# Splitting the last load of V by rows, and exchanging two closing copies, in a decode kernel

## The chip, the cores and the metric

The kernel runs on one core of a Trainium2 chip. The metric is the device time of one execution in microseconds (us). Times inside an execution are counted from its first instruction. TensorE is PE (its weight loads PEld), VectorE is DVE, ScalarE is ACT, GpSimd is POOL, and SyncE, which issues most of the transfers, is SP.

## What is computed

Two blocks of a decoder, mixed by a gate. Block A is attention of one new token over a long cache; block B is a small mixer with an MLP. Cut to what matters here:

```python
# B = 2 batches, one new token each; D = 1024; H = 32 heads of Dh = 128; Sk = 16384 cached positions; bf16
q = (x @ wq).reshape(B, 1, H, Dh).transpose(0, 2, 1, 3)
p = softmax(einsum("bhqd,bhkd->bhqk", q, k_cache) * Dh ** -0.5)
a = einsum("bhqk,bhkd->bhqd", p, v_cache).transpose(0, 2, 1, 3).reshape(B, 1, H * Dh) @ wo
b = mixer_and_mlp(x)                     # weights of 2, 2, 7 and 7 MB
g = sigmoid((x * gate_w).sum(-1, keepdims=True))
out = g * a + (1 - g) * b                # (2, 1, 1024)
```

The two caches are 256 MB each, and every byte is used once.

## The kernel before, in words

A **unit** is one batch `s` (0 or 1) with a pair of heads `i` (0 to 15). Its K, and its V, is one load of 8 MB: 128 rows of 65536 bytes, row p holding 256 positions one after the other (256 "columns" of 128 values each). A loop over `i` (line 895) does both batches: SP loads K of this pair, V of the pair before, and one block of `wo`, each as soon as the place in SBUF is free; VectorE transposes K in chunks (line 640), PE multiplies them with the queries (line 663), ScalarE takes the exponents (line 685), and PE multiplies these with V (`pv_moving`, line 713). The sums are brought into shape by VectorE and PE (`dve_rows`, lines 781 and 787; line 731) and are multiplied with `wo` by `add_rows` (line 758) into two accumulators in PSUM, `arow[0]` and `arow[1]`, one for each half of the 1024 output columns.

Each transfer tells of its landing on a semaphore; a transfer raises it by 16 in all. SP issues its transfers in program order, into one queue.

After the loop (lines 926 to 1025) only the V of the last pair is left. The order is written out by hand:

- SP loads V of batch 0 (line 934, 8 MB), then V of batch 1 in four pieces of 128, 64, 48 and 16 columns (lines 937 to 942; all 128 rows of each). The last piece has 4096 bytes in a row, 512 KB in all. Behind it come three loads of `wo`: line 946 (2048 bytes a row), line 947 (1024 bytes, for `arow[1]`) and line 948 (1024 bytes, for `arow[0]`; its semaphore is `l_wl`).
- PE works on the first two pieces with V as the moving operand (lines 983 to 987), and on the last two with V as the weights, a matmul for each column, 48 + 16 (lines 993 to 1000). Ahead of each piece it waits for its semaphore; `landing(n)` is the count, 32 for all of them (16 from an earlier use of the semaphore, and 16).
- VectorE scales the result (line 1002). PE adds it to `arow[0]` and `arow[1]` with eight matmuls of `add_rows` (lines 1005 and 1006), waits for line 947's load and adds four more to `arow[1]`, which is then complete (line 1008), waits for `l_wl` and adds four to `arow[0]` (line 1010).
- ScalarE copies `arow[1]` to `out_row` (line 1013), VectorE copies `arow[0]` (line 1015), and when both are done ACT issues the output transfer (line 1017). POOL waits for that and closes the kernel (lines 1020 to 1025).

```python
PIECES = [128, 64, 48, 16]
...
for n, size in enumerate(PIECES):
    SP.dma_start(
        out=region(V_CELL, NJ * Dh)[:, at * Dh : (at + size) * Dh],
        in_=unit_rows(v_rows, HP - 1, 1)[:, at * Dh : (at + size) * Dh],
    ).then_inc(S(landed[n + 1]), 16)
    at += size
```

Of the kernel before, what the change touches and what calls it, by code (L numbers as in the profile page):

```python
# [10 lines left out]
ACTF = mybir.ActivationFunctionType  # L11
# [77 lines left out]
def kernel(  # L89
# [16 lines left out]
    P = nc.NUM_PARTITIONS  # L106
    B, Sq, D = A_x.shape
    _, H, Sk, Dh = A_k_cache.shape
# [6 lines left out]
    HP = H // 2  # L115
    HALF = P // 2
    NJ = 2 * Sk // P
# [4 lines left out]
    Q4 = 4  # L122
# [14 lines left out]
    def sb(shape, dtype, name):  # L137
        return const.tile(shape, dtype, name=name)
# [3 lines left out]
    def S(name):  # L142
        if name not in sems:
            sems[name] = (tc if name in ("fin", "st") else nc).alloc_semaphore(name)
        return sems[name]
# [48 lines left out]
    out_row = sb([P, NQ], BF16, "out_row")  # L194
# [5 lines left out]
    arow = [psum.tile([P, Dh], FP32, name=f"arow{h}") for h in range(2)]  # L200
# [4 lines left out]
    def region(cell, elements):  # L205
        return mem[:, cell * CELL : cell * CELL + elements]

    K_CELL = (0, 1)
    V_CELL = 3

    k_rows = A_k_cache.rearrange("b (g t) s d -> b g (t s d)", t=2)
    v_rows = A_v_cache.rearrange("b (g t) s d -> b g (t s d)", t=2)
    wo_rows = A_wo.rearrange("(g p r) n -> g (p r n)", p=WP, r=WR)

    def unit_rows(rows, hp, s):
        if isinstance(hp, int):
            flat = rows[s, hp : hp + 1, :]
        else:
            flat = rows[s, bass.ds(hp, 1), :]
        return flat.rearrange("o (p x) -> (o p) x", p=P)  # L220
# [7 lines left out]
    def wait(engine, name, value):  # L228
        if isinstance(value, int) and value == 0:
            return  # L230
        engine.wait_ge(S(name), value)
# [7 lines left out]
    with tc.tile_critical(no_gpsimd_drain=True):  # L239
        PE, DVE, ACT, POOL, SP = nc.tensor, nc.vector, nc.scalar, nc.gpsimd, nc.sync  # L240
# [10 lines left out]
        for b, row in enumerate((A_x[0, 0], A_x[1, 0], gate_w)):  # L251
# [9 lines left out]
                out=ident_f[:], in_=ident_f[:], compare_op=ALU.not_equal, fill=1.0, base=0,  # L261
# [10 lines left out]
        for k in range(2):  # L272
# [14 lines left out]
                out=lmat[:].rearrange("p (g h k) -> p g h k", h=2, k=4),  # L287
                in_=hm2[:].unsqueeze(1).unsqueeze(3).to_broadcast([P, P // 8, 2, 4]),
# [3 lines left out]
        for h in range(2):  # L292
            at = QP + h * (HB // 2)
# [3 lines left out]
                    out=place[:, at : at + P].rearrange("p (g k) -> p g k", k=2 * QP)[:, :, 0 : HB + 1 : HB],  # L297
                    in_=ident_f[:, h * HALF : (h + 1) * HALF].rearrange("p (g k) -> p g k", k=QP)[:, :, 0:B],
# [6 lines left out]
                out=ident_s[:], in0=ident_f[:], scalar1=-scale, scalar2=None, op0=ALU.mult  # L305
# [6 lines left out]
                out=rep1[:], in_=ident_f[:].rearrange("p (c k) -> p k c", k=QP), axis=AX.X, op=ALU.add  # L312
# [6 lines left out]
                out=mask4[:], in_=ident_f[:].rearrange("p (c k) -> p c k", k=QP), axis=AX.X, op=ALU.add  # L319
# [3 lines left out]
        for g in range(Q4):  # L323
# [3 lines left out]
                    out=rep4[:, g, :].rearrange("p (a k) -> p a k", k=QP),  # L327
# [13 lines left out]
                out=hsel[:], in_=rep1[:, 0:8].rearrange("p (h k) -> p h k", k=4), axis=AX.X, op=ALU.add  # L341
# [179 lines left out]
        def linear(actT, w, R, N, act_key, w_key, banks, out_keys):  # L521
# [7 lines left out]
            def one(n):  # L529
# [19 lines left out]
                out=tsc[:],  # L549
                in_=oacc2[:].rearrange("p a (m k e) -> p (a m) e k", k=QP, e=2),  # L550
# [6 lines left out]
                out=qTb[:], in_=tsc[:].rearrange("p (c k) -> p c k", k=QP)[:, :, 0:B]  # L557
# [15 lines left out]
        for e in range(2):  # L573
            rows = slice(e * HALF, (e + 1) * HALF)
# [3 lines left out]
                    out=qd[rows],  # L578
                    in_=R_ps[rows].rearrange("p (hp e v b) -> p e hp b v", e=2, v=4, b=B)[:, e],
# [142 lines left out]
        def v_view(cell):  # L722
            return region(cell, NJ * Dh).rearrange("p (j d) -> p j d", d=Dh)
# [105 lines left out]
        for key in ("qd", "mask4", "qw0", "qw1"):  # L829
# [20 lines left out]
                out=tsc[:, 0:FQ],  # L850
                in_=oacc2[:, :, 0:half].rearrange("p a (i c) -> p c a i", c=FC),
# [34 lines left out]
                out=brow[:], in0=brow[:], scalar1=omgrow[:, 0:1], scalar2=None, op0=ALU.mult  # L886
# [38 lines left out]

        landed = [f"l_{x}" for x in ("wq", "w1", "w2", "xr0", "xr1", "w3", "w4")]

        def landing(n):
            return 32

        PIECES = [128, 64, 48, 16]
        WIDE = 2
        wait(SP, "tr3", 2 * HP)
        SP.dma_start(out=region(0, NJ * Dh), in_=unit_rows(v_rows, HP - 1, 0)).then_inc(S(landed[0]), 16)
        wait(SP, "pvd", 2 * HP - 1)
        at = 0
        for n, size in enumerate(PIECES):
            SP.dma_start(  # L938
                out=region(V_CELL, NJ * Dh)[:, at * Dh : (at + size) * Dh],
                in_=unit_rows(v_rows, HP - 1, 1)[:, at * Dh : (at + size) * Dh],  # L940
            ).then_inc(S(landed[n + 1]), 16)
            at += size
        wo_heads = A_wo.rearrange("(h d) n -> d h n", d=Dh)
        wo_l = region(2, 2 * D).rearrange("p (e n) -> p e n", e=2)
# [20 lines left out]
                out=rinv2[:], in0=rinv2[:], scalar1=g_rep[:, 1:2], scalar2=None, op0=ALU.mult  # L965
# [14 lines left out]
        V = v_view(V_CELL)  # L980
        moving = sum(PIECES[:WIDE])
        j = 0
        for n in range(WIDE):
            wait(PE, landed[n + 1], landing(n + 1))
            ins = pv_moving(V, 1, j // 4, (j + PIECES[n]) // 4, moving // 4)
            j += PIECES[n]
# [5 lines left out]
        PE.matmul(last, lhsT=red[:, 0, :], rhs=hsel[:], start=True, stop=False)  # L992
        for n in range(WIDE, len(PIECES)):
            wait(PE, landed[n + 1], landing(n + 1))
            for _ in range(PIECES[n]):
                ins = PE.matmul(  # L996
                    last, lhsT=V[:, j, :], rhs=pts[1][:, j // 4, :, j % 4], start=False, stop=(j == NJ - 1)
                )
                j += 1
        ins.then_inc(S("otd"), 1)  # L1000
        wait(DVE, "otd", 2 * HP)
        DVE.tensor_tensor(out=OTl[:, :, HB], in0=last, in1=rinv2[:], op=ALU.mult).then_inc(S("OTd"), 1)
        wait(PE, "OTd", 2 * HP)
        wait(PE, landed[-2], landing(-2))
        for h in range(2):
            add_rows(0, OTl, wo_l, h)
# [2 lines left out]
        wait(PE, "l_wl", 16)  # L1009
        add_rows(1, OTl, wo_l, 0, True).then_inc(S("wod"), 1)  # L1010
        used = slice(0, P - HB + 1)
        wait(ACT, "wod", HP + 1)
        ACT.activation(out=out_row[used, Dh : 2 * Dh], in_=arow[1][used, :], func=ACTF.Copy).then_inc(S("fin"), 1)
        wait(DVE, "wod", HP + 2)
        DVE.tensor_copy(out=out_row[used, 0:Dh], in_=arow[0][used, :]).then_inc(S("fin"), 1)
        wait(ACT, "fin", 2)
        ACT.dma_start(
            out=out.rearrange("b s (h g c) -> g (b s) h c", h=2, g=Q4), in_=out_row[0 : P - HB + 1 : HB, :]
        ).then_inc(S("st"), 16)
        used = sorted(sem.num for name, sem in sems.items() if name not in ("fin", "st"))  # L1020
# [35 lines left out]
```

## Time and profile before

| What | us |
|---|---|
| median of 3 runs | 1331.39 |
| their range | 1331.32 to 1331.53 |
| the profiled execution's own time | 1331.36 |
| its span, first to last instruction | 1329.6 |
| PE busy in it | 826.6 |
| VectorE busy | 711.4 |
| ScalarE busy | 105.2 |
| POOL busy | 15.9 |

Read 572.53 MB from HBM over the span, 431 GB/s. The page gives each engine's busy time, the queues of the DMA engines (q1 is SP's, q10 is ACT's, q8 and q14 fetch instructions), and the chain of work that ended last; further answers of the trace give the timeline and the DMA rows of a stretch of the span. In a row of the timeline the columns are the start, the time from the first start to the last end, the engine and line, the operation, and in brackets how long the engine had been idle and what ended that. Beside these the trace keeps a record of every DMA packet (start, duration, bytes, queue, but not which of the 16 DMA engines moved it) and of every semaphore update. SP's queue has one packet for each row of a load.

### The profile page before, as it was taken

To read this page: it belongs to the slowest core of one execution; us is meant where nothing else is said; L and a number is where in the kernel's file an instruction comes from. 1 tells how busy PE (TensorE), PEld (TensorE's weight loads), DVE (VectorE), ACT (ScalarE), POOL (GpSimd) and SP (SyncE) were. 2 spreads that over 40 slices of the span, in tenths; PEclk is the share of its full clock that TensorE was granted. 3 is DMA by queue.
4 is the path that set the end of the run, shared out by engine and by line. 5 is a ranking of instruction groups with operands and counts; after the bars stand their busy time and mean duration, and the time that the engine had idled before them with its cause. 6 is when DMAs were issued, how large, how long until landed. Compare 5 with 4: busy or idle time off the path is not lost.

```text
span 1329.6 us, 14078 instructions
## 1 busy us (share of the span) xinstructions
PE 826.6 (62%) x6060; PEld 378.3 (28%) x6060; DVE 711.4 (54%) x712; ACT 105.2 (8%) x165; POOL 15.9 (1%) x47
## 2 busy tenths in 40 slices
PE   2356576565666656567665657656566775656765
PEld 0123232232332323233232323223232322323323
DVE  2365465654556654456565455665455656545561
ACT  0010000000000000000000000000000000000000
POOL 0100000000000000000000000000000000000000
PEclk9677887777888777788877788877788887778886
DMA  9999999999999999999999999999999999999998
GB/s 410 439 420 436 443 426 440 428 430 436 432 436 432 436 430 442 426 442 426 442 426 442 424 442 426 442 426 433 434 430 438 430 436 432 440 428 440 428 440 346
DMA packets 11573, 572.68 MB, mean 431 GB/s; under 512 B 1472, under 2 KB 1740, under 8 KB 1996
## 3 DMA queue, kind: packets, MB, share of 16 engines
q1 hardware_dynamic: 11520, 572.53, 99.6%
q8 instruction: 8, 0.13, 0.0%
q10 hardware_dynamic: 44, 0.01, 0.0%
q14 instruction: 1, 0.01, 0.0%
HBM read 572.53 MB, written 0.00 MB: 431 GB/s over the span
## 4 chain that ended last, share of the span: by engine, by line
DMA 68%; DVE 14%; PE 13%; issue 3%; another core or an unknown queue 1%; POOL 0%; SPq 0%; POOLq 0%; ACT 0%
DMA mem<-in_A_k_cache_dram 66%; DVE kt L640 14%; PE S L663 12%; DMA mem<-in_A_v_cache_dram 2%; PE oacc L713 0%; PE ot L531 0%; SPq L906 0%; PE R L996 0%; POOL qw L267 0%; POOL pt L269 0%; SPq L938 0%; PE arow L758 0%; DVE st L647 0%; POOL ln_rstd L471 0%
## 5 line engine op out<-in xcount | busy, mean ns | idle before, releaser
L663 PE MATMUL S<-kt,qw 128*128 128x512 bf16 x2048 | 552.1, 420 | 261.7 <-DVE kt L640 261.4
L640 DVE STREAM_TRANSPOSE kt<-mem 128x2048 f32<-128x2048 f32 x256 | 571.6, 2284 | 171.1 <-DMA mem<-in_A_k_cache_dram 115.6
L663 PEld LDWEIGHTS S<-kt,qw 128*128 128x128 bf16 x2048 | 197.9, 105 | 602.1 <-issue 301.3
L713 PE MATMUL oacc<-mem,pt 128*8 128x512 bf16 x2032 | 118.3, 386 | 5.7 <-DMA mem<-in_A_v_cache_dram 5.7
L685 ACT ACTIVATE pt<-st,nb 64x256 bf16<-64x256 f32 x64 | 90.1, 1407 | 279.0 <-DVE nb L699 278.5
L731 PE MATMUL ot<-hsel,red 128*128 128x2 f32 x480 | 71.1, 279 | 54.7 <-DVE red L787 54.7
L731 PEld LDWEIGHTS ot<-hsel,red 128*128 128x128 f32 x480 | 68.5, 224 | 69.9 <-DVE red L787 69.9
L781 DVE TENSOR_SCALAR part<-oacc,maskr 128x128 f32<-128x128 f32 x31 | 10.9, 351 | 140.3 <-PE oacc L713 140.3
L674 ACT ACTIVATE Dm<-ident_s,m 128x128 f32<-128x128 f32 x32 | 12.8, 401 | 878.7 <-DVE m L649 878.7
L704 PE MATMUL R<-rs,lmat 128*128 128x1 f32 x64 | 18.4, 357 | 79.1 <-ACT pt L685 79.1
L713 PEld LDWEIGHTS oacc<-mem,pt 128*8 128x8 bf16 x2032 | 46.9, 87 | 64.8 <-DMA mem<-in_A_v_cache_dram 6.8
L708 DVE RECIPROCAL rinv<-R 128x1 f32<-128x1 f32 x32 | 5.4, 168 | 109.6 <-PE R L704 109.5
L647 DVE STREAM_TRANSPOSE st<-S 128x512 f32<-128x512 f32 x32 | 22.9, 717 | 70.1 <-PE S L663 70.1
L676 PE MATMUL R<-Dm,ones_f 128*128 128x128 f32 x64 | 15.6, 326 | 54.4 <-ACT Dm L674 54.4
L814 DVE TENSOR_SCALAR oa<-ot,hm 128x8 f32<-128x8 f32 x30 | 6.8, 226 | 73.9 <-PE ot L731 73.9
L704 PEld LDWEIGHTS R<-rs,lmat 128*128 128x128 f32 x64 | 15.9, 307 | 84.9 <-ACT pt L685 84.7
L758 PE MATMUL arow<-wo,OT 128*17 128x128 bf16 x960 | 28.3, 310 | 10.5 <-DVE OT L819 10.5
L685 ACT ACTIVATION_READ_ACCUMULATOR pt<-st,nb 64x1 f32 x64 | 30.7, 479 | 0.0
L676 PEld LDWEIGHTS R<-Dm,ones_f 128*128 128x128 f32 x64 | 9.5, 188 | 70.3 <-ACT Dm L674 70.3
L758 PEld LDWEIGHTS arow<-wo,OT 128*17 128x17 bf16 x960 | 24.6, 133 | 11.3 <-issue 11.3
L787 DVE SCALAR_TENSOR_TENSOR part<-oacc,maskr,part 128x128 f32<-128x128 f32 x62 | 21.8, 351 | 2.2
L624 POOL TENSOR_TENSOR qw<-qd,mask 128x16 bf16<-128x16 f32 (+1 forms) x32 | 8.3, 262 | 1118.7 <-PE S L663 1118.7
(114 smaller groups left out, 130.0 us busy)
## 6 DMA issues: line engine op xcount, KB each, us to landing
mem<-in_B_w_dram SPq DMA_DIRECT2D x2, 7168.0 KB, 34.4
wo<-in_A_wo_dram SPq DMA_DIRECT2D x15, 512.0 KB, 24.8
mem<-in_B_w_dram SPq DMA_DIRECT2D x2, 2048.0 KB, 28.5
mem<-in_A_v_cache_dram SPq DMA_DIRECT2D x1, 4096.0 KB, 20.8
mem<-in_A_v_cache_dram SPq DMA_DIRECT2D x1, 2048.0 KB, 25.3
mem<-in_A_v_cache_dram SPq DMA_DIRECT2D x1, 1536.0 KB
mem<-in_A_k_cache_dram SPq DMA_DIRECT2D x32, 28.3
mem<-in_A_v_cache_dram SPq DMA_DIRECT2D x1, 512.0 KB
```

What stands on the lines that cost most here:

```text
L640: DVE.transpose(out=kt[n % 2][:], in_=k_view(s)[:, c * CT : (c + 1) * CT, :].rearrange("p j d -> p (j d)").bitcast(FP32),).then_inc(S(f"tr ...
L647: DVE.transpose(out=st[:].rearrange("p j r -> p (j r)"), in_=sps[s][:]).then_inc(S("stT"), 1)
L663: ins = PE.matmul(sps[s][:].rearrange("p (j k) -> p j k", k=QP), lhsT=qw[s][:, v, NG - 1 - m : NG - 1 - m + P], rhs=ktb[:, half * GT : (ha ...
L674: ACT.activation(out=Dm[:], in_=ident_s[:], func=ACTF.Copy, scale=m_t[:, 0:1]).then_inc(S("dm"), 1)
L676: PE.matmul(R_ps[:, 0:P], lhsT=ones_f[:], rhs=Dm[:], start=True, stop=True).then_inc(S("rr"), 1)
L685: ins = ACT.activation(out=pts[s][rows, :, e, :].rearrange("p (m a) k -> p a k m", a=GT // 4), in_=st[rows, :, 0:NG].rearrange("p (a k) m ...
L704: PE.matmul(tot_ps[:, 0:1], lhsT=lmat[:], rhs=rs_t[:], start=True, stop=True).then_inc(S("tt"), 1)
L713: ins = PE.matmul(oacc[s][QP * q : QP * q + 8, :], lhsT=pts[s][:, g].rearrange("p h k -> p (h k)"), rhs=V[:, 4 * g : 4 * g + 4, :].rearran ...
L731: ins = PE.matmul(ot_ps[:, 2 * r : 2 * r + 2], lhsT=red_t[:, r : r + 2 * P - 1 : 2], rhs=hsel[:], start=True, stop=True, skip_group_check= ...
L758: ins = PE.matmul(arow[h][QP * g : QP * g + HB + 1, :], lhsT=o[:, e, :], rhs=w[:, e, at : at + Dh], start=False, stop=stop, skip_group_che ...
L781: ins = DVE.tensor_scalar(out=part[:], in0=in0, scalar1=mask[:, 0:1], scalar2=None, op0=ALU.mult)
L787: ins = DVE.scalar_tensor_tensor(out=red[:] if twice else part[:], in0=in0.unsqueeze(1).to_broadcast([P, 2, Dh]) if twice else in0, scalar ...
```

## The change

The last piece of V, 16 columns, comes in five loads instead of one: one of rows 0 to 111, and four of 4 rows each, rows 112 + k, 116 + k, 120 + k and 124 + k for k = 0 to 3. PE waits on their common semaphore for 96 (16 from its earlier use, and 5 times 16). And the closing copies change engines: VectorE copies `arow[1]`, which is complete first, and ScalarE copies `arow[0]`. The number of columns in each piece, the matmuls and the output transfer stay as they are; SP has four issues more, and the order of each engine's other instructions is the same.

```diff
-        def landing(n):
-            return 32
-
         PIECES = [128, 64, 48, 16]
         WIDE = 2
+        LAST, FEW = len(PIECES) - 1, 4
+        def landing(n):
+            return 16 * (2 + FEW) if n == LAST + 1 else 32
+
         wait(SP, "tr3", 2 * HP)
         SP.dma_start(out=region(0, NJ * Dh), in_=unit_rows(v_rows, HP - 1, 0)).then_inc(S(landed[0]), 16)
         wait(SP, "pvd", 2 * HP - 1)
         at = 0
         for n, size in enumerate(PIECES):
-            SP.dma_start(
-                out=region(V_CELL, NJ * Dh)[:, at * Dh : (at + size) * Dh],
-                in_=unit_rows(v_rows, HP - 1, 1)[:, at * Dh : (at + size) * Dh],
-            ).then_inc(S(landed[n + 1]), 16)
+            rows = [slice(0, P)]
+            if n == LAST:
+                rows = [slice(0, P - Q4 * FEW)] + [slice(P - Q4 * FEW + k, P, FEW) for k in range(FEW)]
+            for r in rows:
+                SP.dma_start(
+                    out=region(V_CELL, NJ * Dh)[r, at * Dh : (at + size) * Dh],
+                    in_=unit_rows(v_rows, HP - 1, 1)[r, at * Dh : (at + size) * Dh],
+                ).then_inc(S(landed[n + 1]), 16)
             at += size
...
         used = slice(0, P - HB + 1)
-        wait(ACT, "wod", HP + 1)
-        ACT.activation(out=out_row[used, Dh : 2 * Dh], in_=arow[1][used, :], func=ACTF.Copy).then_inc(S("fin"), 1)
-        wait(DVE, "wod", HP + 2)
-        DVE.tensor_copy(out=out_row[used, 0:Dh], in_=arow[0][used, :]).then_inc(S("fin"), 1)
+        wait(DVE, "wod", HP + 1)
+        DVE.tensor_copy(out=out_row[used, Dh : 2 * Dh], in_=arow[1][used, :]).then_inc(S("fin"), 1)
+        wait(ACT, "wod", HP + 2)
+        ACT.activation(out=out_row[used, 0:Dh], in_=arow[0][used, :], func=ACTF.Copy).then_inc(S("fin"), 1)
         wait(ACT, "fin", 2)
```

## The prediction

> **What bounds the kernel now.** I read the page first: the span, the DMA row, the queues.
>
> ```profile
> span 1329.6 us, 14078 instructions
> ...
> DMA  9999999999999999999999999999999999999998
> ...
> q1 hardware_dynamic: 11520, 572.53, 99.6%
> q8 instruction: 8, 0.13, 0.0%
> q10 hardware_dynamic: 44, 0.01, 0.0%
> q14 instruction: 1, 0.01, 0.0%
> ```
>
> The DMA row is 9 in 39 of 40 slices, and SP's queue (q1) fills 99.6% of the time of 16 DMA engines. The kernel is a stream of 572.53 MB, and the change leaves the bytes as they are. Only what follows the stream's last bytes can move the end. So the second view is the end of the chain of work (asked from 1240 us on):
>
> ```profile
> 1295.20 28.52 DMA mem<-in_A_v_cache_dram
> 1323.72 0.05 issue
> 1323.76 1.88 PE R L996 x64
> ...
> 1325.89 0.75 PE arow L758 x16
> 1326.64 0.02 issue
> 1326.66 0.30 DVE out_row L1015
> ```
>
> This chain goes through PE: the piece of 48 columns lands at 1323.72 and 64 matmuls run without a break. It hides a second one of almost the same length. The timeline from 1325.5 us shows it:
>
> ```profile
> 1325.89 0.22 PEld L758 LDWEIGHTS arow<-mem,OT_last 128*17 128x17 bf16 x12 [0.34 <-DVE OT_last L1002]
> ...
> 1326.32 0.10 PEld L758 LDWEIGHTS arow<-mem,OT_last 128*17 128x17 bf16 x4 [0.21 <-DMA mem<-in_A_wo_dram]
> 1326.44 0.28 ACT L1013 ACTIVATE out_row<-arow 113x128 bf16<-113x128 f32 x1 [24.48 <-PE arow L758]
> 1326.66 0.29 DVE L1015 CAST out_row<-arow 113x128 bf16<-113x128 f32 x1 [0.83 <-PE arow L758]
> 1326.98 0.62 ACTq L1017 DMA_DIRECT2D out_dram<-out_row  x1
> ```
>
> The last four weight loads sat idle 0.21 us until a DMA of A_wo landed. That is the last load of the kernel (l_wl); the trace's semaphore updates put its last landing at 1326.277. So the end is set by the landing of l_wl, and PE could be at most 0.4 us earlier (its first twelve weight loads start at 1325.89).
>
> The third view is the DMA answer for 1322 to 1327 us, 40 slices of 0.125 us:
>
> ```profile
> DMA  9799989799999989864554545449210000000000
> ```
>
> From about 1324.1 to 1325.5 us the row stands at 4 to 5: half the engines have finished. The sixteen semaphore updates of l_wl say the same: eight from 1324.53 to 1324.84, eight from 1325.57 to 1326.28 (1325.571, 1325.872, 1325.947, 1325.994, 1326.051, 1326.057, 1326.132, 1326.277). The landings of the 16-column piece are split alike: 1323.13 to 1323.47, and 1324.310 to 1324.968. Eight engines are late because of instruction fetches: the packet records show one on q14 (39.2 us, 0.31 us long) and eight on q8 (0.95 to 1.16 us); after each but the last (1325.4, on an engine that had finished) one more engine lands late for good.
>
> **Which engines take the loads of four rows.** The trace of before has four-row loads only on ACT's queue (three at the start). Each gives its semaphore one early update and then four, where a load of 128 rows gives 16. So a load of four rows runs on four engines, a row each. The packets tell which four: on an engine a packet starts 3 or 4 ns before the one ahead ends, so the 11520 packets of q1 can be strung into 16 chains of 720, and the 512-byte packets of those loads (7.4 to 17.4 us) lie in four of them. Three of the four end among the early eight. The fourth took the q14 fetch and is the first of the late eight (1325.571). A tie of 1 ns at 61.6 us leaves one doubt: a second of the four may be the late one that lands second (1325.872).
>
> That SP's four-row loads take the same four engines is not shown. [...]
>
> **The change, part by part.**
> (a) The load of 112 rows: 7 rows an engine instead of 8. A 4096-byte packet takes 0.159 us and the next starts 4 ns before its end, so a row is 0.156 us. Twelve engines lose 0.156 us.
> (b) The four small loads: four engines get 4 rows more, each with a 4-byte semaphore packet (0.006 us from start to start). They have 7 x 0.156 + 0.006 + 4 x 0.162 = 1.746 us instead of 8 x 0.156 + 0.006 = 1.254, so +0.492 us.
> (c) The last landing. If the four are those of ACT's loads, seven of the late eight are 0.156 earlier, the last at 1326.277 - 0.156 = 1326.121. The late one of the four lands l_wl at 1325.571 + 0.492 = 1326.063, the three early ones at 1324.84 + 0.49 = 1325.33 at most. So the last landing moves by **-0.156 us**; all later loads go with it.
> (d) PE: it needs columns 48 to 63 of its 64 at 1325.04, and the piece of 16 had landed at 1324.968; it then lands at 1324.81. No gain there and no loss: the margin grows from 0.07 to 0.23 us. The wait on 96 instead of 32 has the last 16 matmuls behind it, and nothing else earlier. The first two A_wo loads land at 1325.46 (from 1325.616) and 1325.80 (from 1325.957), ahead of 1325.89. The last four matmuls start 0.043 us after l_wl, at 1326.16 instead of 1326.32.
> (e) SP: four more issues. The row by line:
>
> ```profile
> 1294.34 1.76 SPq L938 DMA_DIRECT2D mem<-in_A_v_cache_dram  x4
> 1296.15 0.43 SPq L946 DMA_DIRECT2D mem<-in_A_wo_dram  x1
> ```
>
> An issue is 0.43 us and the next follows 0.04 later, so SP is 4 x 0.47 = 1.9 us later with the three loads of A_wo. Their first packets run at 1322.6, 24 us after the new issue: hidden by the queue ahead. Without that cover it would be 1.9 us.
> (f) The exchange. Both copies start 0.050 us after their last matmul's end (1326.389 to 1326.440, 1326.610 to 1326.660). ScalarE's takes 0.277 us, VectorE's 0.292, and the later one is on the path: -0.015. From VectorE's end to ACT's output load it is 0.032 us. From ScalarE's own end to its own queue no row shows; the nearest are ScalarE to PE, 0.052 (1290.200 to 1290.252), and 0. So the exchange is worth between -0.05 and +0.01; I take -0.015, the handover being one semaphore as before. VectorE has nothing behind its wait; ACT has only the output load behind it, which needed both halves anyway.
> Sum: -0.156 - 0.015 = **-0.17 us**, and the rest (output load 1.7 us, the closing barriers) moves along. The profiled execution took 1331.36 us with a span of 1329.6; it becomes 1331.19. The median of the three runs is 0.03 above it: 1331.22. The runs spread over 0.21 us, so this is hardly more than the noise.
>
> **The rivals.**
> *The four loads don't gather.* If each small load takes four engines of its own, every engine has 8 rows as before, plus one semaphore packet: 1331.39 - 0.015 + 0.006 = 1331.38. For it: no trace shows SP's choice. Against it: the three loads of ACT's queue all went to the same four. That would be the change not doing what it says.
> *A late engine among the four.* The work added is 0.492 us, and it decides as soon as one of the four has less slack than that to the last landing at 1326.277. The second late one has 0.405, so the end moves by +0.09: 1331.46. Of the last three late ones (slack 0.22 to 0) it would be +0.27 to +0.49: 1331.65 to 1331.87. This is **slower than before**. For it: the tie at 61.6 us, and that a fetch may land elsewhere (one comes at 1310.4, 13 us before this stage). Against it: the chains as strung.
> *Each small load waits out the one before.* A lone small transfer, the output, is issued at 1326.98 and landed at 1328.70: 1.72 us. Four in a row on the same engines would be 6.9 us: 1338.3. For it: all four go to the same engines. Against it: on q1 the next load's first packet starts 6 ns after the start of the semaphore packet ahead, everywhere. [...]
>
> **How the numbers follow.** Forecast 0.56; not gathered 0.10; a late engine 0.24 (half of it the small case); waiting out 0.03; anything else 0.07. Time: 1331.2. The range has to hold the forecast with a run's spread (1331.0) and the late engine with all of its price (1331.87): 1330.95 to 1331.9; only waiting out and part of the rest stay outside. 0.2% of this kernel, 2.7 us, is about what a measurement of it can tell from no change. All cases but the waiting out and a part of the unknown lie within it: same 0.93, slower 0.05, faster 0.02.
>
> **What would show it.** In the trace after: 12 engines land the last piece 0.156 us earlier, and the last updates of l_wl come near 1326.12; the idle time ahead of the last four weight loads of L758 falls from 0.21 us; ScalarE's copy ends about 1326.78, and the output load is issued near 1326.81. Wrong would be: last landing at or after 1326.28, a gap between the small loads' packets, or more than 0.06 us between the end of ScalarE's copy and the issue.

## The result, and the profile after

The change made the kernel **slower by 1.95 us**: 1333.49 us (median of 22 runs, 1333.26 to 1334.03) against 1331.54 (22 runs of the kernel before on the same chip, 1331.22 to 1332.58). The ratio is 1.0015, with a 95% interval from 1.0009 to 1.0021. The profiled execution took 1333.51 us. The forecast was 1331.2, and the range, 1330.95 to 1331.9, does not hold the result.

The page after, its span and SP's queue:

```profile
span 1331.6 us, 14082 instructions
...
q1 hardware_dynamic: 11536, 572.53, 99.6%
```

The same 572.53 MB took 2.0 us more, in 16 more packets: each small load adds 4 semaphore packets of 4 bytes. The share of 99.6% did not fall, so the DMA engines were as busy as before in a longer span: no idle time came in, the packets themselves became longer (their time summed and divided by 16 rose from 1324.71 to 1326.77 us, by 2.06).

The end of the chain of work after (columns: start, duration, what):

```profile
1297.86 29.34 DMA mem<-in_A_v_cache_dram
1327.20 0.05 issue
1327.24 0.60 PE R L1001 x16
...
1328.09 0.64 PE arow L758 x16
1328.73 0.02 issue
1328.75 0.28 ACT out_row L1020
```

Before, the last DMA on the chain was the piece of 48 columns, landed at 1323.72; now it is the piece of 16, landed at 1327.20 instead of 1324.97. The timeline has, of before, PE's weight loads for the last 64 columns:

```profile
1323.76 1.78 PEld L996 LDWEIGHTS R<-pt,mem 128*128 128x128 bf16 x64 [0.40 <-DMA mem<-in_A_v_cache_dram]
```

and, after, the same stretch to the end:

```profile
1325.32 1.36 PEld L1001 LDWEIGHTS R<-pt,mem 128*128 128x128 bf16 x48 [1.98 <-DMA mem<-in_A_v_cache_dram]
...
1327.24 0.51 PEld L1001 LDWEIGHTS R<-pt,mem 128*128 128x128 bf16 x16 [0.56 <-DMA mem<-in_A_v_cache_dram]
...
1328.09 0.36 PEld L758 LDWEIGHTS arow<-mem,OT_last 128*17 128x17 bf16 x16 [0.34 <-DVE OT_last L1007]
1328.65 0.29 DVE L1018 CAST out_row<-arow 113x128 bf16<-113x128 f32 x1 [0.61 <-PE arow L758]
1328.75 0.28 ACT L1020 ACTIVATE out_row<-arow 113x128 bf16<-113x128 f32 x1 [27.18 <-PE arow L758]
1329.06 0.62 ACTq L1022 DMA_DIRECT2D out_dram<-out_row  x1
```

PE now stands idle 1.98 us ahead of the 48 columns (0.40 before) and 0.56 us ahead of the 16, where it had run on without a break. The load of 48 columns, which the change does not touch and which is queued *ahead* of the split one, lands 1.56 us later. The last landings, by the semaphore updates (us):

| load | before | after |
|---|---|---|
| 128 columns / 64 columns | 1315.125 / 1320.027 | 1315.122 / 1320.013 |
| 48 columns | 1323.717 | 1325.278 |
| 16 columns | 1324.968 | 1327.198 |
| the first two loads of `wo` | 1325.616, 1325.957 | 1327.646, 1327.987 |
| `l_wl` | 1326.277 | 1328.310 |

So the loss begins between 1320 and 1325 us. The DMA answer for 1320 to 1328 us shows it, in 40 slices of 0.2 us. Its first row is the busy share of the 16 engines in tenths, its second the GB/s that they moved. Before:

```profile
DMA  9799993998999699999976464547100000000000
GB/s 614 307 430 430 430 492 164 471 410 348 532 410 399 246 389 389 348 440 384 369 246 241 154 230 169 179 164 200 36 5 0 0 0 0 0 0 0 0 0 0
```

After:

```profile
DMA  5998969799399929997499899997976657544300
GB/s 246 553 430 369 553 266 430 287 451 328 82 348 225 307 61 318 246 184 133 87 210 236 205 282 292 220 210 154 184 123 113 174 179 261 200 174 169 113 31 10
```

From 1322 to 1324 us (the 11th to the 20th number) the mean falls from 391 to 199 GB/s, while the busy row goes on showing mostly 9. Both rows count a packet whole in the slice in which it starts, which is where the row's 2 to 4 come from; spread over their durations, the packets fill all 16 engines from 1320 to 1325.4 us in the run after. So the engines hold packets all the time, and each packet takes longer (spread likewise, 407 and 228 GB/s from 1322 to 1324 us). The packet records, one duration for each packet of SP's queue:

| packets, us | before | after |
|---|---|---|
| 4096 bytes (16 columns), median / longest | 0.160 / 0.172 | 0.263 / 0.425 |
| of these 128, over 0.2 us | 0 | 111 |
| 12288 bytes (48 columns), longest | 0.474 | 0.969 |
| 2048 bytes (first load of `wo`), median | 0.084 | 0.1355 |

The first long packets (12288 bytes, 0.487 us) start at 1321.29 us. The earliest engines began the load of 112 rows at 1321.18, while the others were still at the 48 columns. Packets of the loads ahead and behind are stretched as well, though those loads have 128 rows as before.

### The profile page after: what moved, and what is told of

The parts are those of the page before. It is cut to its first block, busy times and chain, and to the rows that moved or that the text cites. A ratio compares the mean times of both kernels' runs of the same rounds, so it can differ in the third digit from the quotient of the medians.

```text
span 1331.6 us, 14082 instructions
## 1 busy us (share of the span) xinstructions
PE 825.1 (62%) x6060; PEld 375.1 (28%) x6060; DVE 711.3 (53%) x712; ACT 105.2 (8%) x165; POOL 15.9 (1%) x47
## 3 DMA queue, kind: packets, MB, share of 16 engines
q1 hardware_dynamic: 11536, 572.53, 99.6%
HBM read 572.53 MB, written 0.00 MB: 430 GB/s over the span
## 4 chain that ended last, share of the span: by engine, by line
DMA 68%; DVE 15%; PE 12%; issue 3%; another core or an unknown queue 1%; SPq 0%; POOL 0%; ACT 0%; POOLq 0%
DMA mem<-in_A_k_cache_dram 66%; DVE kt L640 14%; PE S L663 12%; DMA mem<-in_A_v_cache_dram 2%; PE ot L531 0%; SPq L943 0%; PE oacc L713 0%; SPq L906 0%; POOL qw L267 0%; POOL pt L269 0%; DVE st L647 0%; POOL ln_rstd L471 0%; PE arow L758 0%; PE R L1001 0%
## 5 line engine op out<-in xcount | busy, mean ns | idle before, releaser
L731 PE MATMUL ot<-hsel,red 128*128 128x2 f32 x480 | 68.0, 272 | 54.7 <-DVE red L787 54.7
L731 PEld LDWEIGHTS ot<-hsel,red 128*128 128x128 f32 x480 | 65.5, 215 | 69.9 <-DVE red L787 69.9
```

The costliest lines, as they stand in the source:

```text
L731: ins = PE.matmul(ot_ps[:, 2 * r : 2 * r + 2], lhsT=red_t[:, r : r + 2 * P - 1 : 2], rhs=hsel[:], start=True, stop=True, skip_group_check= ...
```

## The experiments

Each kernel ran in 10 timed executions, beside 19 to 31 of the kernel before on the same chip. The difference is that of the two medians. Single runs scatter by some 0.2 us and the intervals of the ratios are about 0.1% (1.3 us) to either side, so a difference of 0.5 us is no proof alone; landings and packets of the profiled execution are given beside it. All kernels but the first contain the exchanged copies.

**What was to be told apart.** Besides the exchange: (i) the number of loads in the queue (theory C in the expectations); (ii) uneven work, the four small loads piling up on four engines (theory B); (iii) the load of 112 rows, by where it reads in HBM (theory D); (iv) the load of 112 rows, by which rows of SBUF each engine writes (theory A).

**The exchange alone.** The kernel before with only the closing copies exchanged.

> The loads as before, only the two copies exchanged. Theory A (the loss is all in the loads: with 112 rows an engine no longer writes the rows that it writes in a load of 128, and several engines then write into the same part of SBUF and share its rate), theory B (the loss is that the four loads of 4 rows pile up on four engines), theory C (the loss comes with the number of loads in the queue) all say: 1331.5, no difference that can be timed, -0.015 us in the trace, and 0.03 us from the end of ScalarE's copy to the issue of the output load. Only if the exchange itself costs (a rival) would it be +0.5 us or more.

Measured: 1331.58 us against 1331.58, ratio 1.0000 (0.9990 to 1.0009). Its timeline at the end:

```profile
1326.44 0.29 DVE L1013 CAST out_row<-arow 113x128 bf16<-113x128 f32 x1 [0.61 <-PE arow L758]
1326.67 0.28 ACT L1015 ACTIVATE out_row<-arow 113x128 bf16<-113x128 f32 x1 [25.07 <-PE arow L758]
1326.97 0.62 ACTq L1017 DMA_DIRECT2D out_dram<-out_row  x1
```

ScalarE's copy ends at 1326.945 and its own queue issues 0.030 us later. From the landing of `l_wl` to that issue it is 0.687 us, and 0.707 before: the exchange gains 0.02 us. All of the loss comes from the loads.

**Number of loads, uneven work, the large load alone.** Three edits of the list of rows:

```diff
-                rows = [slice(0, P - Q4 * FEW)] + [slice(P - Q4 * FEW + k, P, FEW) for k in range(FEW)]
# 112 rows and one load of 16 rows
+                rows = [slice(0, P - Q4 * FEW), slice(P - Q4 * FEW, P)]
# 112 rows alone (the last 16 columns of rows 112 to 127 are not loaded)
+                rows = [slice(0, P - Q4 * FEW)]
# five loads of all 128 rows, of 12, 1, 1, 1 and 1 columns
+            widths = [12, 1, 1, 1, 1] if n == LAST else [size]
```

> After, but rows 112 to 127 in one load of 16 rows: every engine again has 8 rows, 7 and 1. Theory A: still slow, +1.3 to +2.2 us over before, and 4096-byte packets of 0.2 to 0.4 us in place of 0.159. Theory B: the pile-up is gone, 1331.5, packets of 0.16 us. Theory C: two loads in place of five, +0.5 us at most.

> After without the four small loads: rows 112 to 127 of the last 16 columns are left out, and old values stand there. Theory A: the packets still stretch, to 0.2 to 0.4 us for 4096 bytes and up to 0.9 us for 12288; +0.7 to +1.7 us over before. Theory B and theory C: an eighth of the piece less and nothing piled up, -0.17 us, packets of 0.159 us.

> The last piece in five loads of all 128 rows (12, 1, 1, 1 and 1 columns): as many loads in the queue as after, and no rows split off. Theory A and B: +0.1 to +0.3 us (32 packets of 256 bytes an engine at some 0.015 us in place of a quarter of the 4096-byte ones), and the landing of the 48 columns stays at 1323.7. Theory C: +2 us, as after.

| kernel | this / before, us | ratio (95%) | 4096-byte median / longest | over 0.2 us | `l_wl` landed |
|---|---|---|---|---|---|
| 112 and 16 rows | 1333.41 / 1331.58 | 1.0014 (1.0004 to 1.0024) | 0.255 / 0.431 | 111 of 128 | 1328.327 |
| 112 rows alone | 1332.93 / 1331.58 | 1.0011 (1.0001 to 1.0021) | 0.266 / 0.451 | 91 of 112 | 1327.775 |
| five loads of 128 rows | 1331.90 / 1331.58 | 1.0002 (0.9993 to 1.0012) | no such packet | | 1326.461 |

With one load of 16 rows in place of the four small ones the loss is there as before (1.83 us); that every engine then has 8 rows again was my estimate, and which engines took the 16 rows is not shown. The load of 112 rows alone, 7 rows to an engine by the chains of packets of the run after, loses as well, with nothing piled up: it is not uneven work. Five loads as such cost 0.32 us by the medians and 0.18 by the landing of `l_wl`, in small packets (256 bytes took 0.018 us); the longest of the 12288-byte packets there is 0.472, as before: it is not the number of loads. The load of 112 rows alone costs 1.35 us, though it moves 64 KB *less*; the four small ones add the other 0.6. In that run PE's wait for the 48 columns is:

```profile
1324.88 1.36 PEld L1001 LDWEIGHTS R<-pt,mem 128*128 128x128 bf16 x48 [1.58 <-DMA mem<-in_A_v_cache_dram]
```

1.58 us idle instead of 0.40: the load queued behind slows the one ahead.

**Source or destination.** All 16 columns in four loads of 32 rows, once rows that lie 4 apart, once neighbours; and 112 rows read from one unbroken stretch of HBM (which gives other values of V in them).

```diff
# 32 rows, 4 apart
+                rows = [slice(k, P, FEW) for k in range(FEW)]
# 32 neighbouring rows
+                rows = [slice(32 * k, 32 * k + 32) for k in range(FEW)]
# 112 rows (alone) from one stretch
+                src = unit_rows(v_rows, HP - 1, 1)[0:8, :].rearrange("q (m x) -> (q m) x", x=size * Dh)
```

> The last piece in four loads of 32 rows that lie 4 apart over all 128 rows, as the loads of A_wo in the loop, whose 16384-byte packets run at 0.611 to 0.622 us, the pace of 128 rows. Theory A (several engines write into one part of SBUF and share its rate): rows spread like this reach every part, each engine keeps the part that it writes otherwise, so no stretching: packets of 0.159 us, 1331.6. Theory A' (any load of other than 128 rows among loads of 128 stretches them): +1.3 us or more. Theory D (the reads from HBM collide when 112 rows are read): 1331.6 too, since every row is read in loads of equal size.

> The same, but the four loads take 32 neighbouring rows each (0 to 31, 32 to 63 and so on). Same bytes, same number of loads, rows and engines. Theory A: sixteen engines now write into half of the parts or fewer at a time, so packets of 4096 bytes of 0.3 us or more, and +1 to +2.5 us over before. A theory of counts (rows, loads, bytes) has to give the same time as for the rows 4 apart.

> As the run with 112 rows alone, but the 112 rows of 4096 bytes are read one behind the other from HBM in place of 65536 bytes apart; so the last 16 columns hold other values than they should, and rows 112 to 127 old ones. Theory A: the reads don't matter, +1.35 us over before as with 112 rows alone (1332.93), packets of 0.2 to 0.45 us. Theory D: no stretching, packets of 0.159 us, -0.17 us.

| kernel | this / before, us | ratio (95%) | 4096-byte median / longest | over 0.2 us | `l_wl` landed |
|---|---|---|---|---|---|
| 32 rows, 4 apart | 1331.57 / 1331.57 | 0.9999 (0.9989 to 1.0009) | 0.159 / 0.167 | 0 of 128 | 1326.321 |
| 32 neighbours | 1333.58 / 1331.57 | 1.0014 (1.0005 to 1.0024) | 0.2555 / 0.328 | 111 of 128 | 1328.254 |
| 112 rows, one stretch | 1333.05 / 1331.57 | 1.0012 (1.0003 to 1.0022) | 0.264 / 0.508 | 98 of 112 | 1327.916 |

The first two have the same bytes, the same number of loads and the same number of landings (the answers for 1320 to 1328 us count 128 packets under 512 bytes in both, 16 for each of eight loads, and 80 before, for five); only which rows stand together in a load differs. The same answer as above, 1320 to 1328 us, for the rows 4 apart:

```profile
GB/s 369 614 307 430 369 553 287 369 492 287 430 369 492 338 359 328 405 379 430 364 302 261 266 179 195 261 184 138 46 10 0 0 0 0 0 0 0 0 0 0
```

and for the neighbours:

```profile
GB/s 614 307 614 369 307 553 184 512 287 471 205 205 102 246 287 348 92 205 195 195 236 292 302 220 241 195 236 266 225 143 133 143 118 246 174 184 154 92 36 0
```

From 1322 to 1324 us that is 389 against 208 GB/s. Reading the 112 rows from one stretch of HBM changes nothing (a median of 0.264 us for the 4096-byte packets, 0.266 with the rows 65536 bytes apart), so how the source lies in HBM is not it.

That leaves the rows of SBUF that a load writes. Theory A is a guess about them: an engine is quick in the rows that it writes in a load of 128, and slow in others. Which rows those are for an engine no run shows, as a packet's record tells neither its engine nor its row; where the expectations speak of an engine's part, they mean the rows so guessed, and the lower and the upper half are rows 0 to 63 and 64 to 127. The next runs put the guess to the test.

**A few rows, in one place or another.** The load of 128 rows stays whole. Behind it come four extra loads of 4 rows, read again from V into a place in SBUF that nothing uses; PE waits for them too. From run to run the rows differ, those written in SBUF and with them those read from V (that the source matters was ruled out for 112 rows only); one run has a single extra load.

```diff
# behind the load of 128 rows; r is one of the lists below
+                SP.dma_start(out=spare[r], in_=unit_rows(v_rows, HP - 1, 1)[r, at * Dh : (at + size) * Dh]
+                             ).then_inc(S(landed[n + 1]), 16)
# 112, 116, 120, 124 (+k)   slice(P - Q4 * FEW + k, P, FEW)
# 0, 4, 8, 12 (+k)          slice(k, Q4 * FEW, FEW)
# 112 to 115 (+4k)          slice(P - Q4 * FEW + 4 * k, P - Q4 * FEW + 4 * k + 4)
# 4, 8, 12, 16 (+k)         slice(Q4 + k, Q4 + Q4 * FEW, FEW)
# 112, 116, 120, 124 once   for k in range(1)
# 32, 64, 16 (+4j+k)        slice(32 + k, 32 + Q4 * FEW, FEW), and with 64 and 16
```

> The last piece in one load of 128 rows, as before, and behind it four extra loads of 4 rows that lie 4 apart (rows 112 + k, 116 + k, 120 + k, 124 + k again), into a place of SBUF that nobody uses; PE waits for them too. 64 KB more than before. Theory A: the four engines write into parts that four others also write: 16 packets somewhat stretched (0.16 to 0.32 us), all else as before, +0.1 to +1.0 us. Theory B (the pile-up on four engines, four rows of 0.162 us each, 0.65 us, of which a late engine with 0.70 us of slack takes all): 0 to +0.1 us, or up to +0.65 us if another late engine is among the four.

> As the run with four extra loads of 4 rows, but the extra rows are k, 4 + k, 8 + k and 12 + k in place of 112 + k and so on: the same number of loads, rows and bytes, the same four engines, another place in SBUF. [...] Theory B (the load on the four engines, wherever they write) and a theory of counts: as with rows 112 to 127, 1332.24.

> As the run with four extra loads of rows 4 apart in 112 to 127, but each extra load takes 4 neighbouring rows of these (112 to 115 and so on). Theory A: all four engines and the owner meet in one part at a time, so the extra packets take 3 to 5 times as long, 0.5 to 0.8 us, and the time is more than 1332.24 by 0.5 us or more. Theory B or a theory of counts: 1332.24.

Rows 4 to 19 (4 + k, 8 + k, 12 + k and 16 + k):

> [...] Theory A: it stretches the packets as rows 112 to 127 did: +0.4 to +0.7 us over before, 4096-byte packets of up to 0.3 us. If only the upper rows were slow to write, or only late engines' parts count: 1331.6 and no stretching.

> One extra load of 4 rows (112, 116, 120, 124) in place of four: 4 packets of 4096 bytes, 16 KB. If what is lost is the time of the packets that are written into another engine's part, a quarter of the 0.67 us: +0.1 to +0.2 us. If one such packet holds up the whole stream until its end, +0.5 us or more.

> Four extra loads of 4 rows, 32 + k, 36 + k, 40 + k and 44 + k. [...] If only the rows 0 to 15 are free for them, +0.4 us or more.

Rows 64 to 79 (64 + k, 68 + k, 72 + k and 76 + k):

> [...] If crossing into the upper half is what stretches the packets of all busy engines: as rows 112 to 127, 1332.24, and sixty or more 4096-byte packets over 0.2 us. If each part is shared only by the two engines that meet in it: a few packets of 0.3 us, +0.1 to +0.5 us.

Rows 16 to 31 (16 + k, 20 + k, 24 + k and 28 + k):

> [...] If crossing the halves is what spreads the stretching: a few packets of 0.3 us only, +0.1 to +0.5 us. If any part of others does it: as rows 112 to 127, 1332.24, with sixty or more packets over 0.2 us.

| rows of the extra loads | difference, us | ratio (95%) | 4096-byte longest | over 0.2 us | `l_wl` landed |
|---|---|---|---|---|---|
| 0, 4, 8, 12 (+k) | -0.06 | 0.9999 (0.9990 to 1.0009) | 0.172 | 0 of 144 | 1326.134 |
| 32, 36, 40, 44 (+k) | -0.03 | 1.0000 (0.9991 to 1.0010) | 0.172 | 0 of 144 | 1326.362 |
| 112, 116, 120, 124, once | -0.01 | 1.0000 (0.9990 to 1.0009) | 0.214 | 5 of 132 | 1326.483 |
| 4, 8, 12, 16 (+k) | +0.46 | 1.0004 (0.9994 to 1.0014) | 0.327 | 7 of 144 | 1326.904 |
| 16, 20, 24, 28 (+k) | +0.49 | 1.0004 (0.9994 to 1.0013) | 0.336 | 43 of 144 | 1326.994 |
| 112 to 115 (+4k) | +0.51 | 1.0003 (0.9993 to 1.0013) | 0.338 | 59 of 144 | 1327.033 |
| 112, 116, 120, 124 (+k) | +0.67 | 1.0005 (0.9996 to 1.0015) | 0.333 | 45 of 144 | 1327.120 |
| 64, 68, 72, 76 (+k) | +0.68 | 1.0005 (0.9996 to 1.0015) | 0.331 | 37 of 144 | 1327.319 |

The DMA answer for 1320 to 1328 us, extra rows 0, 4, 8, 12 (+k):

```profile
GB/s 676 307 430 492 430 369 266 553 389 246 553 369 328 430 318 400 379 451 333 394 338 307 292 277 200 200 210 236 31 0 0 0 0 0 0 0 0 0 0 0
```

and 112, 116, 120, 124 (+k):

```profile
GB/s 369 553 369 430 430 430 287 266 594 348 430 410 440 348 297 338 225 220 179 184 277 302 297 246 251 225 230 195 179 184 190 190 36 5 0 0 0 0 0 0
```

Both move 64 KB more than before. Sixteen more packets cost nothing when they go into rows 0 to 15 or 32 to 47 (-0.06 and -0.03 us, no packet over 0.172 us), where I had estimated 1331.6 us. In rows 112 to 127, 64 to 79 or 16 to 31, 37 to 59 packets take over 0.2 us, up to 0.34. The guess fits that far if rows 0 to 15 and 32 to 47 are those of the engines that carried the extra rows, which no trace shows. The medians' differences of 0.5 to 0.7 lie within the intervals; the trace tells the runs apart more clearly. From the landing of the 64 columns, behind which the kernels differ, to that of `l_wl` it is 6.25 us before, 6.23 to 6.36 in the first three runs of the table, 6.31 with rows 4 to 19, and 6.83 to 7.21 in the last four.

Several expectations missed. The run with rows 112, 116, 120, 124 (+k) was to stretch its 16 extra packets and leave all else as before; 45 were stretched. Four neighbouring rows should have been worse than four apart, with packets of 0.5 to 0.8 us; they were not (0.338). For rows 64 to 79 and 16 to 31 either "sixty or more" or "a few" long packets were expected, and there were 37 and 43. And rows 4 to 19, which were to do as rows 112 to 127, stretched only 7 packets. Nearly all of that run's time came from elsewhere: one engine was 0.57 us late already at the piece of 128 columns (1315.70), and it is one of the two that end last. So its 0.46 us tells little of the rows. One small load in place of four (4 packets) took 0.1 us more between those two landings in the profiled run and nothing in the timed ones, where 0.1 to 0.2 had been expected: the price grows with the number of such packets.

**What stays open.** In the run with rows 112, 116, 120, 124 (+k) all of the eight late engines show packets of 0.28 us and more, though by the chains of packets seven of them carry none of the extra rows (one of the four that do is among the late ones). The early engines that carried no extra rows had finished their 16 columns by then and show none. With rows 64 to 79 and 16 to 31 it is again all eight late ones. So what slows a packet is not only a matter of the engine that carries the extra rows; why the others are held up too is not shown. Nor is it clear why rows 4 to 19 stretch so few packets (7, against 37 to 59), and no run separates it.

## Why the prediction was wrong, step by step

- **(a) is the step that failed:** "A 4096-byte packet takes 0.159 us ... so a row is 0.156 us." That duration was read from loads of 128 rows and carried to a load of 112 rows. There the median was 0.263. In loads of 32 rows 4 apart it is 0.159 as I had it. That 112 rows come 7 to an engine no run of before shows; the chains of packets of after do (twelve of them have 7 packets of 4096 bytes). I counted rows per engine and did not ask which rows; no load of before has 112 rows, so no row showed this price, and it should have been bounded, not taken over. That the length of the packets goes by which rows a load takes together is shown (0.159 us for 32 rows 4 apart, 0.2555 for 32 neighbours), and that for 112 rows the source is not the cause (0.264 from one stretch); by what means the rows written do it is open.
- **(b)** Which engines take the four loads was right, though no run of before shows that they take the same four. Strung into chains of packets, four chains have 11 packets of 4096 bytes and twelve have 7; three of the four end early, and the fourth is the first of the late ones to begin its 16 columns (1322.64). The size was not: 4 x 0.162 = 0.65 us for four rows, in the chains of after about 1.28. One chain each, durations in ns (ties of a few ns leave some places of such a chain open):

```
before                        166 159 159 160 159 159 164 172
after, a chain of seven       162 159 159 200 307 266 262
after, one of the four        166 159 164 232 275 254 262 316 245 401 322
extra rows 0, 4, 8, 12 (+k)   166 159 159 160 159 159 164 172 159 162 159 159
```

- **(c)** fell with (a): the last landing moved by +2.03 us instead of -0.156.
- **(d)** assumed that the 48 columns land as before, because they are ahead in the queue. The sixteen engines do not stand at one place of it: while the late ones still move the 48 columns (landed at 1325.278), the early ones write the split load (from 1321.18). The "margin" of 0.07 us that was to grow became a wait of 0.56.
- **(e)** was hidden as forecast, but the size was off. SP's issues after:

```profile
1293.96 4.47 SPq L943 DMA_DIRECT2D mem<-in_A_v_cache_dram  x8
1298.48 0.44 SPq L951 DMA_DIRECT2D mem<-in_A_wo_dram  x1
```

  The four loads of 4 rows took 0.743, 0.637, 0.577 and 0.576 us to issue, not 0.43: 2.7 us with the gaps instead of 1.9. It goes with the spacing of the rows: four loads of 4 neighbouring rows took 0.255 to 0.379 us each. The loads of `wo` were issued 2.3 us later, with over 20 us of cover left.
- **(f)** was right: -0.02 us in the run with the exchange alone, where -0.015 was taken.
- **The rivals.** "Not gathered" and "waits out the one before" did not happen: the packets follow one another without a gap. "A late engine among the four" has the right sign, but is not what happened: its price, 0.09 to 0.49 us, counts rows on an engine, and the run with 112 rows alone, 7 to an engine and nothing piled up, lost 1.35 us. The case that came true was in none of them.

No version beat the kernel before. The exchange alone, and 32 rows 4 apart, equal it. Of the splits by rows tried here only 32 rows 4 apart kept the packets at 0.159 us. That a late engine's rows can't be handed to an idle one at no cost is my estimate from these runs, and was not tried further.

## What to carry to other kernels

A load's cost is not its bytes and its rows per engine alone: ask which rows of SBUF it takes together, and keep a split load to shapes whose packets keep their length (here 128 rows, 0.160 us at the median, or 32 rows 4 apart, 0.159; 32 neighbours took 0.2555). A duration read from one shape need not hold for another (0.160 us became 0.263). When DMA engines are busy throughout and move half as much (407 and 228 GB/s here), look at the durations of single packets, those of the neighbouring loads too.

## What the runs showed of the hardware

- A load of 112 rows, or of 32 neighbouring rows, made 4096-byte packets take 0.26 us at the median (0.160 before), and 12288-byte packets of another load up to 0.97 us (0.474).
- Sixteen extra packets of 4-row loads into rows 16 to 31, 64 to 79 or 112 to 127 cost 0.5 to 0.7 us by the medians (0.6 to 1.0 by the landings), seven other engines being slowed with them; sixteen into rows 0 to 15 or 32 to 47 cost nothing that shows.
- A load of 4 rows that lie 4 apart took SP 0.58 to 0.75 us to issue, of 4 neighbouring rows 0.26 to 0.38, and of 128 rows 0.34 to 0.43.
